# Attention and two squared-ReLU MLPs on one core: the product of probabilities and values in whole 128-row key blocks

## The chip, the core and the metric

The kernel runs on one core of a Trainium2 chip. Its engines are TensorE (PE in the profile; its weight loads stand as PEld), VectorE (DVE), ScalarE (ACT), GpSimd (POOL) and SyncE (SP), which here issues most of the DMAs. The metric is the device time of one execution in microseconds (us); lower is better.

## The reference

Four batches of eight heads, 576 positions, 64 dimensions per head, all in float32. Attention is causal with a decay, and two MLPs follow, each with 512 inputs, 2048 hidden units and a squared ReLU, over 2304 tokens:

```python
cum = np.cumsum(np.log(np.clip(f, 0.0001, 1.0)), axis=-1)
scores = np.matmul(q, k.transpose(0, 1, 3, 2)) / np.sqrt(D) + cum[:, :, :, None] - cum[:, :, None, :]
scores = np.where(causal, -1000000000.0, scores)
attn = np.exp(scores - np.max(scores, axis=-1, keepdims=True))
attn = attn / (np.sum(attn, axis=-1, keepdims=True) + 1e-09)
x = np.matmul(attn, v)            # then tokens x 512
h = np.maximum(x @ w_in, 0.0); x = h * h @ w_out       # first MLP
r = np.maximum(x @ w_in2, 0.0); out = r * r @ w_out2   # second MLP
```

## The kernel before, in words

The kernel first writes all its work as operations with an engine, an estimated duration, a priority and what they depend on (`op`, line 88), and a list scheduler (`Plan.run`, line 106) simulates the engines and puts out the instructions in the order that it finds. Each engine then works its own queue in that fixed order, with semaphores between them. A change of an estimated duration can therefore change the order on every engine, from the simulated moment on in which the operation is first placed.

The queries of a batch are cut at 0, 64, 192, 320, 448 and 576 (`QB`, line 19). Queries 0 to 191 are done first, in small products (lines 485 to 627). The other 384 queries of a head are one `unit` (line 634), 32 in all, in three query tiles of 128 (t = 2, 3, 4). A unit loads q and k, splits them into high and low parts on ScalarE, VectorE and GpSimd (lines 649 to 665), makes scores on TensorE (line 704), takes the maximum (line 408), the exponential (line 416), normalizes and splits the probabilities into two float16 parts (lines 431 and 438) and lays them out in `ph` as 2 x `NB` blocks of 128 queries by 128 keys, 13 for each part: blocks 0 to 3 for query tile 2, 4 to 7 for tile 3, 8 to 12 for tile 4 (`PB`, line 22). A query tile ends 64 positions into a key block, so its last key block is half used: the upper 64 keys lie after every query of the tile, and the lower 64 after the first 64 queries, whose probabilities there are zero by the mask. `consts_ph` (line 1311) fills the upper halves with zeros once, at the start. A DMA from the queue of SyncE (line 722) transposes all blocks into `pt`, of which there is one buffer (`npt=1`): keys on partitions, queries along the free side.

`av` (line 727) multiplies the values with them. The values are in `vv` as three bfloat16 parts; the first two stand side by side as 128 columns of weights, so that one matmul gives both products in the two halves of the output's partitions. For each key block j there are "cuts": the half block of the query tile for which j is the last (64 rows, 64 to 128 of its query columns), and the full block for all later query tiles (128 rows). Each cut is one matmul with the high and one with the low part of the probabilities. Then the cuts are taken once more for the third part of the values with the high part of the probabilities alone: 64 columns of weights, which write to the lower or the upper 64 partitions of the output, as `THIRD` (line 26) says. The values of keys 576 to 639 are zeros (line 1467). All add up in one PSUM bank; ScalarE and VectorE add its halves into `X` (line 752).

The first MLP (`hidden`, line 850; `mlp_a`, line 888) takes groups of 256 tokens, sixteen pieces of the hidden units each: 12 matmuls of 256 columns per piece for the first product (line 848) and 12 for the second (line 923). These fill TensorE between the heads' products, and go on alone when the last head is done. From the end of attention on, VectorE, ScalarE and GpSimd prepare the second MLP's weights (lines 1043 to 1116), which TensorE then works (lines 1220 and 1246).

The steps that matter most below are the transpose (`o_tr`, line 724: after the probabilities, with a free `pt`) and the product (`o_av`, line 750: after the transpose and the values, holding `pt`, `vv` and the output bank).

Of the kernel before, what the change touches and what calls it, by code (L numbers as in the profile page):

```python
# [18 lines left out]
QB = [0, 64, 192, 320, 448, 576]  # L19
Q0, QA = QB[1:3]  # L20

PB = {2: 0, 3: 4, 4: 8}
NB = 13
MW = 448

THIRD = ((0, 0), (1, 1), (3, 1), (5, 0), (2, 0), (4, 0), (6, 1))
S15 = 2.0 ** -15


# [40 lines left out]
class Plan:  # L70
# [17 lines left out]
    def op(self, eng, dur, fn, prio, deps=(), uses=(), data=None, other=None, dmas=1, rows=128):  # L88


        o = Op()
        o.how, o.uses, o.data, o.dmas, o.rows, o.turn = {eng: (dur, fn, 0)}, tuple(uses), data, dmas, rows, dur == self.TURN[0]
        if other:
            o.how[other[0]] = (other[1], other[2], 1)
        o.prio = (prio, len(self.ops))
        o.outs, o.ready, o.nwait = [], 0.0, 0
        for d in deps:
            if d is not None:
                d.outs.append(o)
                o.nwait += 1  # L100
        for b in o.uses:
            b.left += 1
        self.ops.append(o)
        return o
# [122 lines left out]
def act(n, psum=False):  # L227
    return (0.052 if psum else 0.093) + 0.00083 * n
# [6 lines left out]
def dve2(n):  # L235
    return Port(0.07 + n / 1920.0)
# [26 lines left out]
def attention_then_two_squared_relu_mlps(  # L263
# [16 lines left out]
    B, H, D2, S = qk.shape  # L280
# [10 lines left out]
    op = P.op  # L291
# [66 lines left out]
    def groups(c0, c1):  # L358
        return range(max(c0, 0) // GA, (c1 - 1) // GA + 1)
# [82 lines left out]
    def v_parts(vv, n, prio, dep):  # L442


        def rest(eng, i):
            x = vv()[:, :, i]
            eng.tensor_tensor(out=vv()[:, :, 1] if i == 0 else x.bitcast(BF16)[:, :, 0::2], in0=x,  # L447
                              in1=x.bitcast(BF16)[:, :, 1::2], op=ALU.subtract)

        for i in range(2):  # L450
            dep = either(TUNE["vr"], ("POOL", pool_(n * D), lambda i=i: rest(nc.gpsimd, i)),
                         ("DVE", dvs(n * D), lambda i=i: rest(nc.vector, i)), prio, [dep], [vv_of[vv]])
        return dep
# [180 lines left out]
    def unit(b, h, prio, first):  # L634

        c = QA
        qk_ = [Buf(QK), Buf(QK)]
        ta, tb = qk_
        raw, vv, ph, pT, o = Buf(RAW), Buf(VV), Buf(PH), Buf(PT), Buf(BO)
# [50 lines left out]
        ov = op("SP", P.COPY[0], load_v, prio + TUNE["vd"], [ld], [vv], data=0.91)  # L690
        ov = v_parts(vv, 5, prio + TUNE["vd"], ov)

        p_ops = []
        for t, blk in PB.items():
            pp = Buf(PP)
            q0, wd = QB[t], QB[t + 1]
            cuts = [(0, wd)] if wd <= 512 else [(0, wd // 2), (wd // 2, wd)]
# [26 lines left out]
        o_tr = op("SP", P.TURN[0], tr, prio, p_ops + (a_av if b == 0 else []), [ph, pT], data=2.9)  # L724


        def av():
            x, w_, z = pT(), vv().bitcast(BF16), o()
            cuts = []
            for j in range(5):  # L730
                if j >= 2:
                    cuts.append((j, min(128, QB[j + 1] - 128 * j), slice(128 * j - QA, QB[j + 1] - QA), (slice(PB[j] + j, PB[j] + j + 1), slice(64, 128))))
                t = max(2, j + 1)
                if t <= 4:
                    cuts.append((j, 128, slice(QB[t] - QA, S - QA), (slice(PB[t] + j, PB[4] + j + 1, 4), slice(0, 128))))
            todo = []
            for j, rows, q, (n, c) in cuts:
                for z0 in range(0, 2 * NB, NB):
                    todo.append((z[:, q], w_[:rows, j].rearrange("p z d -> p (z d)")[:, 1::2], x[:rows, n.start + z0:n.stop + z0:n.step or 1, c]))
            for i, half in THIRD:  # L740
                j, rows, q, (n, c) = cuts[i]
                todo.append((z[64 * half:64 * half + 64, q], w_[:rows, j, 1, 0::2], x[:rows, n.start:n.stop:n.step or 1, c]))
            for i, (dst, lt, rh) in enumerate(todo):
                nc.tensor.matmul(dst.rearrange("p (n c) -> p n c", n=rh.shape[1]), lhsT=lt, rhs=rh, start=(i == 0), stop=(i == len(todo) - 1),  # L744
                                 skip_group_check=True)


        p0, p1 = pos(b, QA), pos(b, QA) + S - QA
        gone = [y for g in groups(p0 - RING, p1 - RING) for y in split_x_ops[g][h // 2]] if p1 > RING else []
        o_av = op("PE", 2.06, av, prio, [o_tr, ov] + gone, [pT, vv, o])  # L750

        def fold(eng):
            s = p0
# [516 lines left out]
    with tc.manual_schedule():  # L1270
# [46 lines left out]
        def f_clip(a, z):  # L1317
            nc.vector.tensor_scalar(out=f_in[:, a:z], in0=f_in[:, a:z], scalar1=1.0e-4, scalar2=1.0, op0=ALU.max, op1=ALU.min)

        def f_ln(a, z):  # L1320
            nc.scalar.activation(out=f_log[:, a:z], in_=f_in[:, a:z], func=AF.Ln)
# [42 lines left out]
        o = op("SP", P.COPY[0], f_load, U, data=0.2)  # L1364
# [9 lines left out]
        o = op("DVE", dve2(Q0), lambda: f_clip(0, Q0), U, [o_f])  # L1374
        o = op("ACT", act(Q0), lambda: f_ln(0, Q0), U, [o])
# [7 lines left out]
        o = op("DVE", 0.67, scan1, -1.0e7, [o_f])  # L1383
# [22 lines left out]
        for h in range(H):  # L1406
            unit(0, h, TUNE["BP0"] + TUNE["BP1"] * h, [step(TUNE["P10"] + TUNE["P11"] * h)] if TUNE["P10"] >= 0 else [])
        mlp_a(3)
        for h in range(H):
            unit(1, h, 4500.0 + 100.0 * h, [step(TUNE["P20"] + TUNE["P21"] * h)])  # L1410
        mlp_a(4)
        mlp_a(5)
        for h in range(H):
            unit(2, h, 6000.0 + 100.0 * h, [step(TUNE["P30"] + TUNE["P31"] * h)])
# [19 lines left out]
        gone, taken, far = [[] for _ in RIGHT], [], []  # L1434
        waiting, sums = None, []
        for u in range(NU):
# [14 lines left out]
            gone = [[x] for x in prods]  # L1451
# [55 lines left out]
```

## Time and profile before

| | before |
|---|---|
| time, median of 3 runs | 990.28 us (989.86 to 993.13) |
| span of the profiled execution | 990.6 us |
| TensorE busy | 966.4 us (98%), 6699 matmuls |
| VectorE busy | 687.9 us (69%) |
| ScalarE busy | 452.7 us (46%) |
| GpSimd busy | 340.2 us (34%) |
| line 744 (`av`) on TensorE | 77.7 us, 672 matmuls |
| mean granted clock of TensorE | 0.985 of 2.4 GHz |

The profiled execution's span agrees with the median to 0.3 us. Busy time counts an engine as busy while any of its instructions runs. Matmuls are pipelined: the next one starts before the one ahead of it has ended, so the durations of single matmuls can't be added up, and the distance from start to start is what one costs. A line of the timeline gives a start, the length from there to the end of the last of its matmuls, and how many there are; looked at through a narrow window it gives the start of a single matmul.

### The profile page before, as it was taken

To read this page: it belongs to the slowest core of one execution; us is meant where nothing else is said; L and a number is where in the kernel's file an instruction comes from. 1 tells how busy PE (TensorE), PEld (TensorE's weight loads), DVE (VectorE), ACT (ScalarE), POOL (GpSimd) and SP (SyncE) were. 2 spreads that over 40 slices of the span, in tenths; PEclk is the share of its full clock that TensorE was granted. 3 is DMA by queue.
4 is the path that set the end of the run, shared out by engine and by line. 5 is a ranking of instruction groups with operands and counts; after the bars stand their busy time and mean duration, and the time that the engine had idled before them with its cause. 6 is when DMAs were issued, how large, how long until landed. Compare 5 with 4: busy or idle time off the path is not lost.

```text
span 990.6 us, 17537 instructions
## 1 busy us (share of the span) xinstructions
PE 966.4 (98%) x6699; PEld 864.2 (87%) x6699; DVE 687.9 (69%) x1351; ACT 452.7 (46%) x890; POOL 340.2 (34%) x278
## 2 busy tenths in 40 slices
PE   5999999999999999999999999999999999999997
PEld 3788898788888888888899999888898989899886
DVE  6989667767677777777378689979684445745343
ACT  2775577767677776766333344132231102311011
POOL 2211253444444344444222445343342213522220
PEclk6999999999999999999999999999999999999999
DMA  9766145656657655755557712863352211322223
GB/s 268 241 194 215 64 109 115 146 106 145 137 110 148 143 121 107 164 106 117 119 159 229 228 40 86 273 219 107 128 161 106 74 64 65 106 86 82 67 65 106
DMA packets 172948, 131.92 MB, mean 133 GB/s; under 512 B 134784, under 2 KB 151424, under 8 KB 170688
## 3 DMA queue, kind: packets, MB, share of 16 engines
q1 hardware_dynamic: 172608, 130.32, 48.4%
q8 instruction: 52, 0.85, 0.3%
q10 hardware_dynamic: 256, 0.49, 0.2%
q14 instruction: 32, 0.26, 0.1%
HBM read 85.07 MB, written 18.42 MB: 104 GB/s over the span
## 4 chain that ended last, share of the span: by engine, by line
PE 74%; issue 8%; DVE 7%; DMA 4%; POOL 2%; ACT 2%; SPq 1%; POOLq 0%; DVEq 0%; ACTq 0%
PE hp L848 17%; PE yp L923 16%; PE hp L1220 12%; PE bk L1246 10%; PE bk L744 7%; PE yp L1246 5%; PE bk L704 4%; POOL g L1233 2%; DVE w L1109 1%; DMA st<-in_w_dram 1%; PE bk L617 1%; DMA w<-wo_d 1%; PE bk L577 1%; DMA ph<-in_w_dram 1%; PE bk L619 1%
## 5 line engine op out<-in xcount | busy, mean ns | idle before, releaser
L923 PE MATMUL yp<-gt,w 128*128 128x256 f32 x1728 | 229.6, 282 | 1.6 <-POOL gt L873 1.6
L848 PE MATMUL hp<-xk,w 128*128 128x256 f32 x1728 | 225.9, 281 | 0.0
L923 PEld LDWEIGHTS yp<-gt,w 128*128 128x128 f32 x1728 | 215.9, 189 | 3.4 <-POOL gt L873 2.0
L848 PEld LDWEIGHTS hp<-xk,w 128*128 128x128 f32 x1728 | 213.6, 188 | 1.0 <-DVE xk L542 0.2
L873 POOL TENSOR_TENSOR gt<-sq,gt 128x512 fp32r<-128x512 f32 x72 | 100.1, 1390 | 202.2 <-ACT gt L870 189.0
L1246 PE MATMUL bk<-w,g 128*128 128x512 f32 x576 | 148.3, 394 | 0.4 <-DMA w<-wo_d 0.2
L1233 POOL TENSOR_TENSOR g<-r,g 128x768 fp32r<-128x768 f32 x36 | 66.6, 1851 | 212.1 <-ACT g L1232 210.3
L1220 PE MATMUL hp<-w 128*128 128x384 f32 x630 | 123.8, 335 | 0.3 <-DVE st L1197 0.3
L1232 ACT CAST g<-r 128x768 fp32r<-128x768 f32 x47 | 39.3, 836 | 184.1 <-DVE r L1231 184.0
L1246 PEld LDWEIGHTS bk<-w,g 128*128 128x128 f32 x576 | 106.6, 188 | 18.3 <-POOL g L1233 0.6
L1220 PEld LDWEIGHTS hp<-w 128*128 128x128 f32 x630 | 111.6, 188 | 8.3 <-DVE st L1197 0.7
L416 ACT ACTIVATE pp<-pp,stat 128x448 f32<-128x448 f32 (+1 forms) x128 | 78.5, 614 | 42.8 <-DVE stat L408 34.8
L438 DVE SCALAR_TENSOR_TENSOR ph<-pp,stat,ph 128x320 f16<-128x320 f32 (+2 forms) x96 | 76.2, 798 | 13.9 <-ACT ph L431 12.7
L1197 DVE TENSOR_TENSOR r<-hp,st 128x384 f32<-128x384 f32 x62 | 34.4, 555 | 66.1 <-PE hp L1220 65.6
L744 PE MATMUL bk<-pt,vv 64*128 64x64 f16 (+7 forms) x672 | 77.7, 253 | 0.0
L447 POOL TENSOR_TENSOR vv<-vv 128x320 f32<-128x320 f32 x64 | 55.7, 871 | 55.0 <-DMA vv<-in_v_dram 47.5
L1220 PE MATMUL hp<-w,far 128*128 128x384 f32 x378 | 74.4, 335 | 0.0
L1246 PE MATMUL yp<-w,g 128*128 128x512 f32 x288 | 74.4, 393 | 0.0
L1231 DVE SCALAR_TENSOR_TENSOR r<-r 128x768 f32<-128x768 f32 x47 | 73.0, 1553 | 1.4
L857 ACT ACTIVATE sq<-hp 128x512 f32<-128x512 f32 x72 | 42.9, 596 | 67.4 <-PE hp L848 66.1
L1220 PEld LDWEIGHTS hp<-w,far 128*128 128x128 f32 x378 | 67.3, 188 | 4.9
L744 PEld LDWEIGHTS <-vv 128*128 128x128 bf16 (+3 forms) x672 | 37.1, 101 | 38.8 <-issue 24.9
(174 smaller groups left out, 1269.9 us busy)
## 6 DMA issues: line engine op xcount, KB each, us to landing
w<-wo_d SPq DMA_DIRECT2D x48, 512.0 KB
stage<-in_w_dram SPq DMA_DIRECT2D x26, 512.0 KB
raw<-in_qk_dram SPq DMA_DIRECT2D x32, 288.0 KB
wo_d<-part SPq DMA_DIRECT2D x16, 512.0 KB
st<-in_w_dram SPq DMA_DIRECT2D x7, 1024.0 KB
ph<-in_w_dram SPq DMA_DIRECT2D x7, 1024.0 KB
vv<-in_v_dram SPq DMA_DIRECT2D x32, 160.0 KB
qk_a<-in_qk_dram SPq DMA_DIRECT2D x16, 192.0 KB
```

The source lines that it names most:

```text
L416: nc.scalar.activation(out=x, in_=x, func=AF.Exp, scale=-1.0, bias=nmax[:rows, t:t + 1], accum_out=ssum[:rows, t:t + 1])
L438: nc.vector.scalar_tensor_tensor(out=flat[:rows, z:z + wd], in0=x, scalar=r, in1=flat[:rows, 128 * blk:128 * blk + wd], op0=ALU.mult, op1= ...
L447: eng.tensor_tensor(out=vv()[:, :, 1] if i == 0 else x.bitcast(BF16)[:, :, 0::2], in0=x, in1=x.bitcast(BF16)[:, :, 1::2], op=ALU.subtract)
L744: nc.tensor.matmul(dst.rearrange("p (n c) -> p n c", n=rh.shape[1]), lhsT=lt, rhs=rh, start=(i == 0), stop=(i == len(todo) - 1), skip_grou ...
L848: nc.tensor.matmul(ps, lhsT=lt, rhs=rh, start=(k_ == 0 and c == 0), stop=(k_ == KD - 1 and c == 2))
L857: nc.scalar.activation(out=sq()[:, :c], in_=ps()[:, :c], func=AF.Relu)
L873: eng.tensor_tensor(out=gt[1]()[:, :c], in0=sq()[:, :c], in1=f32(gt[0]()[:, :c]), op=ALU.subtract)
L923: nc.tensor.matmul(yp[d // 2]()[:, d % 2], lhsT=lt, rhs=rh, start=(i == 0 and c == 0 and d % 2 == 0), stop=(i == NF - 1 and c == 2), skip_ ...
L1220: nc.tensor.matmul(ps()[:, 0:TH], lhsT=lt, rhs=rh, start=(k_ == 0 and c == 0), stop=(k_ == 1 and c == 2))
L1231: o = op("DVE", dvs(TU), lambda r=r: nc.vector.scalar_tensor_tensor(out=r(), in0=r(), scalar=0.0, in1=r(), op0=ALU.max, op1=ALU.mult), e0, ...
L1233: l = either_vp(TU, lambda e, r=r, g=g: e.tensor_tensor(out=g()[:, 1], in0=r(), in1=f32(g()[:, 0]), op=ALU.subtract), e0, [h], [r, g])
L1246: nc.tensor.matmul(bank(ob[c]), lhsT=g()[:, a, c * 128:(c + 1) * 128], rhs=rw()[:, b], start=(p == 0 and x == 0 and z == 0), stop=(p == NP ...
```

## The change

A key block's half piece and its full piece become one cut with all 128 rows: key block 2 goes over all 384 query columns, block 3 over the last 256 and block 4 over the last 128. Where a half block has no probabilities, the zeros that lie in `pt` are multiplied. There are five cuts instead of seven kinds of pieces, so a head has 15 matmuls instead of 21. The third part's list is rewritten for the five cuts: blocks 0, 3 and 4 write to the lower 64 partitions, blocks 1 and 2 to the upper ones. The planner is told 1.65 us for the operation instead of 2.06.

```diff
-THIRD = ((0, 0), (1, 1), (3, 1), (5, 0), (2, 0), (4, 0), (6, 1))
+THIRD = ((0, 0), (1, 1), (3, 0), (2, 1), (4, 0))
...
             for j in range(5):
-                if j >= 2:
-                    cuts.append((j, min(128, QB[j + 1] - 128 * j), slice(128 * j - QA, QB[j + 1] - QA), (slice(PB[j] + j, PB[j] + j + 1), slice(64, 128))))
-                t = max(2, j + 1)
-                if t <= 4:
-                    cuts.append((j, 128, slice(QB[t] - QA, S - QA), (slice(PB[t] + j, PB[4] + j + 1, 4), slice(0, 128))))
+                t = max(2, j)
+                cuts.append((j, slice(QB[t] - QA, S - QA), slice(PB[t] + j, PB[4] + j + 1, 4)))
             todo = []
-            for j, rows, q, (n, c) in cuts:
+            for j, q, n in cuts:
                 for z0 in range(0, 2 * NB, NB):
-                    todo.append((z[:, q], w_[:rows, j].rearrange("p z d -> p (z d)")[:, 1::2], x[:rows, n.start + z0:n.stop + z0:n.step or 1, c]))
+                    todo.append((z[:, q], w_[:, j].rearrange("p z d -> p (z d)")[:, 1::2], x[:, n.start + z0:n.stop + z0:n.step]))
             for i, half in THIRD:
-                j, rows, q, (n, c) = cuts[i]
-                todo.append((z[64 * half:64 * half + 64, q], w_[:rows, j, 1, 0::2], x[:rows, n.start:n.stop:n.step or 1, c]))
+                j, q, n = cuts[i]
+                todo.append((z[64 * half:64 * half + 64, q], w_[:, j, 1, 0::2], x[:, n]))
...
-        o_av = op("PE", 2.06, av, prio, [o_tr, ov] + gone, [pT, vv, o])
+        o_av = op("PE", 1.65, av, prio, [o_tr, ov] + gone, [pT, vv, o])
```

## Rows read from the trace of the kernel before

**Rows 1.** The page: the span of the profiled execution.
```profile
span 990.6 us, 17537 instructions
```

**Rows 2.** Busy time by stage: stretch, length, busy us of each engine, clock, DMA.
```profile
165.00:200.00 35.00, 32.72 (x257) 28.38 (x256) 26.26 (x74) 25.87 (x56) 15.88 (x15) 0.95 0.68 138
200.00:475.00 275.00, 274.89 (x2277) 242.10 (x2276) 204.10 (x557) 196.14 (x403) 114.96 (x109) 1.00 0.62 130
492.00:575.00 83.00, 83.00 (x706) 82.96 (x705) 61.50 (x85) 26.70 (x46) 26.14 (x19) 1.00 0.58 185
575.00:620.00 45.00, 43.09 (x330) 41.76 (x330) 40.93 (x53) 22.16 (x34) 23.00 (x15) 1.00 0.24 74
```

**Rows 3.** TensorE's timeline through one head's product: start us, length us, what, count.
```profile
217.95 0.29 PE L704 MATMUL bk<-qk 68*128 68x288 f32 x1
218.09 0.34 PE L744 MATMUL bk<-pt,vv 128*128 128x384 f16 x1
...
218.59 0.33 PE L744 MATMUL bk<-pt,vv 128*128 128x384 f16 x1
218.85 0.23 PE L744 MATMUL bk<-pt,vv 64*128 64x64 f16 x2
219.01 0.28 PE L744 MATMUL bk<-pt,vv 128*128 128x256 f16 x1
219.13 0.27 PE L744 MATMUL bk<-pt,vv 128*128 128x256 f16 x1
219.33 0.39 PE L744 MATMUL bk<-pt,vv 64*128 64x64 f16 x3
219.50 0.29 PE L744 MATMUL bk<-pt,vv 128*128 128x128 f16 x2
219.56 0.38 PE L744 MATMUL bk<-pt,vv 128*128 128x128 f16 x3
219.72 0.23 PE L744 MATMUL bk<-pt,vv 64*128 64x64 f16 x2
219.88 0.35 PE L744 MATMUL bk<-pt,vv 128*64 128x384 f16 x2
220.06 0.28 PE L744 MATMUL bk<-pt,vv 128*64 128x128 f16 x2
220.27 0.25 PE L744 MATMUL bk<-pt,vv 64*64 64x64 f16 x3
220.45 0.39 PE L848 MATMUL hp<-xk,w 128*128 128x256 f32 x1
```

**Rows 4.** Busy time of line 744 alone, whole span: matmuls, weight loads.
```profile
sum 1000.00, PE 77.72 PEld 37.05; mean PE 77.72 PEld 37.05
```

**Rows 5.** TensorE's timeline where whole-array matmuls go over to 64-column ones.
```profile
38.67 0.28 PE L848 MATMUL hp<-xk,w 128*128 128x256 f32 x1
38.90 0.32 PE L617 MATMUL bk<-pt,vv 128*64 128x128 f32 x1
```

**Rows 6.** Groups by line and shape: count, busy us, mean ns, idle before.
```profile
L744 PE MATMUL bk<-pt,vv 64*128 64x64 f16 x192 | 22.1, 196 | 0.0
```

**Rows 7.** Transposes on SyncE's queue, and the start of one head's product.
```profile
220.55 3.99 SPq L722 DMA_TRANSPOSE pt<-ph  x1
231.27 3.93 SPq L722 DMA_TRANSPOSE pt<-ph  x1
317.54 3.94 SPq L722 DMA_TRANSPOSE pt<-ph  x1
325.01 0.34 PE L744 MATMUL bk<-pt,vv 128*128 128x384 f16 x1
```

**Rows 8.** The chain that ended last, around the fourth head: start, length, what.
```profile
170.05 4.20 DMA raw<-in_qk_dram
181.67 2.25 PE hp L848 x12
183.92 2.12 PE yp L923 x12
```

## The prediction

> **What bounds the kernel now.** I began with the span [rows 1] and with busy time by stage [rows 2]. In the attention stage, from 200 to 475 us, TensorE is covered for 274.89 of 275.00 us, VectorE for 204.10 and ScalarE for 196.14. From 492 to 575 us, where only products of the first MLP are left, TensorE has all 83.00 us. From 575 to 620 us it has 43.09 of 45.00 and VectorE 40.93: here the second MLP's weights are prepared, and the two are nearly level. The granted clock is 1.00 in these three, so TensorE runs at 2.4 GHz. In the one stage that the change touches, TensorE's queue is the limit; nothing else is nearer than 204 of 275.
>
> A busy share doesn't tell whether TensorE works or waits inside an instruction, so I next read one head's product of probabilities and values start by start [rows 3]. Its 21 matmuls take from 218.09 to 220.45, 2.36 us. The busy time of line 744, 77.72 us over 672 matmuls [rows 4], is 2.43 us a head for 32 heads; that counts the tail of each head's last matmul, which lies over the next operation's start, so 2.36 stands for all heads. In these 2.36 us the reader is to look at differences between starts:
> - full 128-row matmuls of 384 columns: four starts over 0.50 us (218.09 to 218.59), 0.167 each;
> - the last of them before a 64-row piece: 0.26 (218.59 to 218.85), 0.095 more for the same columns;
> - a pair of 64-row pieces with 64 columns: 0.16 (218.85 to 219.01), 0.17 (219.33 to 219.50), 0.16 (219.72 to 219.88), where the streaming of 128 columns at 0.167 for 384 is 0.06. So each pair carries about 0.1 us as well, on its way back to 128 rows;
> - 256 columns: 0.12 (219.01 to 219.13), and 0.20 (219.13 to 219.33) ahead of a piece; 128 columns: 0.06 and 0.16;
> - the third value part, two 64-column halves of the array at once: 0.18 (219.88 to 220.06) for 384 columns on both halves, then 0.21, then 0.18 for three 64-row pieces.
>
> So 0.095 us is lost at each change of the array's shape, and not where the width changes: scores with 68 rows and 288 columns go over to 128 rows and 384 columns in 0.14 us (217.95 to 218.09, the first two of [rows 3]), which is 288 columns at the same rate and 0.015. From 128 columns of the array to 64 (line 848 to line 617) a matmul of 256 columns takes 0.23 [rows 5] where one like it took 0.12, so that change costs 0.11.
>
> **The change part by part.** *Removed:* three pairs of 64-row pieces and, of the third value part, three pieces; in all nine matmuls of 64 columns a head (the 192 of [rows 6] are six for each of 32 heads, the x3 near the end of [rows 3] is the other three), and with them six of eight changes of shape: to 64 rows and back behind block 1 and behind block 2 (four), the 64 rows between block 3 and the halves (one), and the 64 rows between the halves and the next operation (one). *Added:* zeros. Blocks 2, 3 and 4 take 384, 256 and 128 columns with all 128 rows, where they took 256, 128 and none beside the pieces. *After*, each term from rows 3:
> - blocks 0 to 2, six matmuls of 384 columns, 6 x 0.167 = 1.00;
> - block 3, two of 256: 0.12 as read, or 0.11 by columns (256/384 x 0.167), as the one read stood behind a change; 0.22 for both;
> - block 4, two of 128: 0.06, and 0.16 ahead of a change of shape, 0.22;
> - third part: blocks 0 and 1 on the two halves 0.18; then block 2's 384 columns on one half beside blocks 3 and 4 (256 + 128) on the other. A 384 ahead of a change costs 0.26, and the second matmul on the same half starts about 0.02 late (0.18 against 0.16 of columns): 0.28.
>
> The sum is 1.00 + 0.22 + 0.22 + 0.46 = 1.90 us, 0.46 less than 2.36; 32 x 0.46 = 14.7 us. Bounds: if block 4's matmul on its half starts only when the other half has ended, the last term is 0.18 + 0.16 = 0.34, and with 0.12 and 0.08 for the two uncertain starts a head takes 2.00: 11.5 us. If the 0.167 is really the 0.165 of 218.26 to 218.59 and the change to halves is no dearer than 0.09, a head takes 1.87: 15.7 us. I stay near the middle, since each term has a row of its own shape.
>
> For the 128-column starts the Trainium skill (TensorE: Matmul & The Clock Gate, section "Back-to-back issue gap") gives about 81 ns for each matmul with its weight load. The row shows 0.06 us; by the page's figure the saving would be 0.6 us smaller in all (an estimate, 0.02 x 32), and the row decides.
>
> A rule speaks against the change: the Trainium skill (TensorEngine Tiling (Array Packing), section "Performance Considerations") would keep a contraction of 64 rows as a 64-row tile, two running side by side. Here both pieces of a pair lie on the same 64 rows and start 0.03 to 0.04 us apart, one after the other. If they did run together, that would be worth at most 0.04 x 3 x 32 = 3.8 us to the old form, while its changes of shape would stay, so the rule doesn't turn the sum.
>
> *Where the time goes next.* One transposed buffer serves all heads, so the next head's transpose starts when this product ends: at 220.55, just behind 220.45 [rows 3, 7]. It therefore moves up with the shorter product, and the pitch, 10.72 us from 220.55 to 231.27, becomes 10.26. Between two products TensorE has 10.72 - 2.36, some 8.3 us, of scores and MLP products; the transpose at 317.54 was in use at 325.01, after 7.47 us [rows 7], so it is covered with the same work as before. VectorE's 204.10 of 275.00 [rows 2] would become 78% of a stretch shorter by 4.3%: still cover. The preparation from 492 us starts at the last head's end, and the last group's products move up too, so the level stage of 575 to 620 us moves as a whole; nothing in the program starts at a fixed time. The sum goes against 990.6 us of the profiled execution [rows 1], which is 0.3 us above the median of 990.28: 990.28 - 14.7 = 975.6.
>
> *The planned duration.* The diff also tells the list scheduler 1.65 instead of 2.06 us, and the order on every engine is written from its simulated times. Up to the first head's product nothing moves. Behind it the order is decided by what is ready at the end of that product, and the distances from there are the same, so I expect five MLP products between two heads as now. A cost on its own I put at nothing, with bounds of one stall either way: the only large one in the stage is between the third and the fourth head [rows 8], where a late load (170.05, 4.20 us) made TensorE wait; 35.00 - 32.72 = 2.28 us idle [rows 2], and two products then took 2.25 and 2.12 instead of 1.42 at the lower clock (1.2 GHz; 0.95 is the mean of that stretch), 1.5 us more. One stall is thus 3.8 us.
>
> **The rivals.**
> 1. *New stalls from a shifted order*, one or two of 3.8 us, in the attention stage or where VectorE is level with TensorE (575 to 620 us): 979 to 983. For it: 40.93 of 45.00. Against: the whole stage moves together.
> 2. *The stall before the fourth head vanishes* with the new order: 972. For it, it hangs on one queue order; against, the load follows the transpose and moves up with it.
> 3. *The gap belongs to a change of width, not of shape.* Then 384 to 256 and 256 to 128 still pay 0.095 each, 0.19 x 32 = 6.1 us: 981.7. Against: the 68-row scores, which change width at 0.015.
> 4. *Slower:* the new order leaves four MLP products between two heads instead of five. Then TensorE's cover is 8.3 - 1.4 = 6.9 us (twelve starts of 0.12, [rows 3, 5], are 1.4), and each head waits for its transpose from 0.6 (landing at 7.47) up to 1.3 us (8.2). At 0.6 it takes 24 of the 32 heads, at 1.3 it takes 11, to eat the 14.7 us; if all 32 do, the time is 995 to 1017. Against: the fifth product is taken because it is ready while the transpose is not, and neither time hangs on the product's length.
> 5. *The change doesn't do what it says:* were the zero blocks no longer whole, the count of matmuls at line 744's successor would not fall to 480.
>
> **How the numbers follow.** Forecast (973.5 to 978) 0.70; rival 1 0.14; rival 2 0.08; rival 3 0.03; rival 4 0.03; the rest, an effect I don't see, 0.02. The time is the forecast's, 975.6. The range of 970 to 983 holds the forecast with both bounds of the sum (974.6 to 978.8), rivals 1 and 2, and rival 3. A measurement of this kernel can tell about 0.3% (3 us) from no change: faster 0.94, within it 0.02, slower 0.04.
>
> **What would show it.** In the profile after: 480 matmuls at the product's line, none of 64 rows; starts of a head over 1.87 to 1.95 us; no 0.095 gap between blocks 1 and 2 or 2 and 3, one between block 4 and the halves; pitches of 10.2 to 10.3 us; the last head ending some 15 us sooner, and the start of the second MLP with it. Wrong would be: a head above 2.0 us (the halves serialize, or width matters), or TensorE below full cover between 200 and 475 us (the order shifted).

## The result

The changed kernel takes 977.07 us (median; 976.36 to 977.69) beside 990.59 us for the kernel before (median of four runs): ratio 0.9865, 95% interval 0.9845 to 0.9884. That is 13.5 us less; 975.6 was forecast. The sign, the place and nearly the size are as forecast, but the experiments show that two errors of the prediction partly cancel in this: the product gained 1.4 us more than it said, and what the other engines make of that, and of the planned duration, is not nothing but some 2.6 us.

The page of the changed kernel, its first two rows (three lines of the program fewer, so line 744 is now 741, 848 is 845 and 923 is 920):

```profile
span 975.9 us, 17152 instructions
...
PE 951.1 (97%) x6507; PEld 863.0 (88%) x6507; DVE 681.9 (70%) x1352; ACT 451.5 (46%) x889; POOL 340.1 (35%) x278
```

TensorE has 192 matmuls fewer, six for each of 32 heads. Busy time by stage (stretch, its length, then PE, PEld, DVE, ACT and POOL busy, clock, DMA share, GB/s), to be read beside [rows 2]:

```profile
165.00:200.00 35.00, 35.00 (x288) 32.67 (x288) 27.77 (x78) 27.82 (x58) 16.07 (x15) 1.00 0.71 149
200.00:475.00 275.00, 271.64 (x2172) 248.00 (x2171) 206.14 (x558) 195.16 (x402) 116.10 (x111) 0.99 0.63 129
```

From 165 to 200 us TensorE is now never idle, where 2.28 us were missing. From 200 to 475 us it is idle for 3.36 us, where 0.11 were missing. Over both stretches that is 3.36 us for 2.39: the one large stall of the scores moved from the fourth head to a later one. TensorE's timeline, before and then after (in brackets the idle time ahead of the start, and what ended it):

```profile
181.14 0.54 PE L704 MATMUL bk<-qk 128*128 128x288 f32 x2 [1.93 <-DVE stat L408]
```

```profile
307.33 1.09 PE L704 MATMUL bk<-qk 128*128 128x288 f32 x4 [1.48 <-DVE stat L408]
```

The granted clock is 0.50 (1.2 GHz) behind each of the two, from 182 to 185 us before and from 309 to 312 us after, so this cost moved with the stall.

One head's product, TensorE's timeline through narrow windows (start, length to the end of the last one, what, count), beside [rows 3]:

```profile
202.82 0.34 PE L741 MATMUL bk<-pt,vv 128*128 128x384 f16 x1
...
203.81 0.38 PE L741 MATMUL bk<-pt,vv 128*128 128x256 f16 x2
203.91 0.39 PE L741 MATMUL bk<-pt,vv 128*128 128x256 f16 x3
204.02 0.28 PE L741 MATMUL bk<-pt,vv 128*128 128x128 f16 x2
204.08 0.50 PE L741 MATMUL bk<-pt,vv 128*128 128x128 f16 x3
204.23 0.35 PE L741 MATMUL bk<-pt,vv 128*64 128x384 f16 x2
204.42 0.33 PE L741 MATMUL bk<-pt,vv 128*64 128x256 f16 x3
204.68 0.40 PE L704 MATMUL bk<-qk 128*128 128x288 f32 x1
```

Six matmuls of 384 columns take 0.99 us, two of 256 take 0.21, two of 128 take 0.21, the third part 0.45: 1.86 us from 202.82 to 204.68, where 2.36 stood. Two losses at a change of shape are left, both forecast: the one before the halves, at 204.08 (0.15 for 128 columns, where 0.06 stands ahead of it), and the one from the halves back to the next operation, in the 0.26 from 204.42 to 204.68.

What the transposes and the scores show is not as forecast. Transposes on SyncE's queue, beside [rows 7]:

```profile
388.34 3.93 SPq L722 DMA_TRANSPOSE pt<-ph  x1
398.61 4.30 SPq L722 DMA_TRANSPOSE pt<-ph  x1
...
449.90 4.39 SPq L722 DMA_TRANSPOSE pt<-ph  x1
461.69 3.89 SPq L722 DMA_TRANSPOSE pt<-ph  x1
```

Some pitches are about the forecast's 10.26 us (388.34 to 398.61), others are longer, up to 11.8 (449.90 to 461.69). Counted from the trace, 161 MLP pieces (12 matmuls each) now lie between the first and the last head's product instead of 156; 24 of the 31 gaps have five (27 before), the others three, six or seven. The line of the products and that of the scores, with what the latter waited for (us, times; the waits of matmuls and of weight loads are both counted and overlap, so such lists are compared only with each other), first before, then after:

```profile
L744 PE MATMUL bk<-pt,vv x672: 190/219/352, 151.8 to 491.3; 64*128 64x64 f16 x48, 128*128 128x384 f16 x32, 64*64 64x64 f16 x24, 128*128 128x256 f16 x16
...
  DVE stat L408: 5.3, 5
  DMA qk<-aug_d: 0.9, 2
  DVE qk L665: 0.5, 2
```

```profile
L741 PE MATMUL bk<-pt,vv x480: 218/326/544, 149.9 to 483.6; 128*128 128x384 f16 x64, 128*128 128x256 f16 x32, 128*128 128x128 f16 x32, 128*64 128x256 f16 x32
...
  DVE stat L408: 7.1, 12
  DMA qk<-aug_d: 1.7, 4
  DVE ph L438: 0.6, 1
  DVE qk L665: 0.5, 1
```

The last matmul of the last head's product starts only 7.6 us sooner (491.3 to 483.6), not 15, and 1.9 us of that had passed ahead of the first product (151.8 to 149.9), where the change has no part: from 0 to 149 us the granted clock is 0.92 in the trace of before and 0.95 in the one after. The other traces below begin the first product between 148.8 and 150.9. Set from the first product to the end of the span, the traces differ by 838.8 - 826.0 = 12.8 us. The products account for 32 x 0.50 = 16.1 us of gain; 3.3 us were given back. Of these 0.7 lie inside the products of two heads that were held up (0.4 in the one at 311.5 us, which began at the lower clock), and 2.6 in the distances between other starts from the first to the last product. I call a start late by what its distance from the one ahead of it exceeds the median distance of that pair of lines and shapes in all traces; these sum to 6.7 us before and 9.3 after, 1.5 of the difference at the scores and 1.0 at the MLP's products.

### The profile page after: what moved, and what is told of

It reads as the page before. It is cut to its first block, busy times and chain, and to the rows that moved or that the text cites. A ratio compares the mean times of both kernels' runs of the same rounds, so it can differ in the third digit from the quotient of the medians.

```text
span 975.9 us, 17152 instructions
## 1 busy us (share of the span) xinstructions
PE 951.1 (97%) x6507; PEld 863.0 (88%) x6507; DVE 681.9 (70%) x1352; ACT 451.5 (46%) x889; POOL 340.1 (35%) x278
## 4 chain that ended last, share of the span: by engine, by line
PE 72%; issue 9%; DVE 9%; DMA 3%; POOL 3%; ACT 3%; SPq 1%; POOLq 0%; DVEq 0%; ACTq 0%
PE yp L920 16%; PE hp L845 16%; PE hp L1217 13%; PE bk L1243 10%; PE bk L741 5%; PE yp L1243 5%; PE bk L704 4%; POOL g L1230 2%; DMA st<-in_w_dram 1%; DVE w L1106 1%; PE bk L617 1%; DMA qk<-aug_d 1%; PE bk L577 1%; DVE ph L438 1%; DVE tmp L805 1%
## 5 line engine op out<-in xcount | busy, mean ns | idle before, releaser
L408 DVE CUSTOM_DVE_ANT_0 pp<-bk,mask 128x448 f32<-128x448 f32 (+1 forms) x128 | 59.8, 475 | 13.2 <-PE bk L704 10.2
L857 DVE SCALAR_TENSOR_TENSOR sq<-hp,sq 128x512 f32<-128x512 f32 x64 | 44.0, 688 | 35.2 <-ACT sq L854 34.8
```

Of the source, the lines that this page charges most:

```text
L408: nc.vector.tensor_tensor_reduce(out=x[:rows, c0:c0 + wd], in0=src, in1=msk, scale=-0.125, scalar=3.0e38 if first else nmax[:rows, 5:6], o ...
```

## The experiments

All ratios are against the kernel before, run beside each kernel on its chip. The clock doesn't separate these kernels: the mean granted clock of each one's runs lies between 0.988 and 0.991, which is worth some 2 us between the extremes (an estimate: 0.002 of 980), and in each of the traces of before, after, e1, e2 and e3 it falls to 1.2 GHz once between the first and the last product. The theory that I began with: the product gained all 16.1 us, and the changed order lost some of it. Its rival: the order costs nothing, and the shorter product itself exposes a wait.

### The order of before with the new product, and the reverse

e1 changes only the planned duration of the changed kernel back:

```diff
-        o_av = op("PE", 1.65, av, prio, [o_tr, ov] + gone, [pT, vv, o])
+        o_av = op("PE", 2.06, av, prio, [o_tr, ov] + gone, [pT, vv, o])
```

> The five whole-block cuts, but the planner is told 2.06 us as before, so every engine's order is that of the kernel before. If the part of the gain that is missing (32 heads x 0.50 us are 16.1 us, 13.5 came) was lost to the changed order: a head's product 1.86 us, 156 MLP pieces between the first and the last head as before, no new stalls, 974.5 us, about 2.5 us less than the changed kernel (ratio 0.984). If the missing part belongs to the shorter product itself (less work to cover the next head's transpose): about 977 us, ratio 0.9865, with waits at the products.

Measured: ratio 0.9914 (0.9901 to 0.9927), 980.15 us, a gain of only 8.5 us. A head's product takes 1.86 us and 156 pieces lie between the heads, as in the kernel before. My theory falls: with the old order, more of the gain is lost (7.6 us of 16.1), not less. The list of what the scores waited for in e1:

```profile
  DVE stat L408: 8.6, 17
  DVE qk L665: 4.1, 5
```

VectorE's part is 12.7 us where it was 5.8 (5.3 + 0.5) in the kernel before, in the same order of instructions. Line 408 takes the maximum out of the scores' PSUM bank and so frees it; line 665 copies a part of q. Both stand in VectorE's queue, and TensorE now comes back to the scores half a microsecond sooner after each head.

e2 has the kernel before with 1.65 us planned:

```diff
-        o_av = op("PE", 2.06, av, prio, [o_tr, ov] + gone, [pT, vv, o])
+        o_av = op("PE", 1.65, av, prio, [o_tr, ov] + gone, [pT, vv, o])
```

> The old cuts with 64-row pieces, but the planner is told 1.65 us, so the order is that of the changed kernel. If the changed order costs time by itself: a head's product still 2.36 us, 161 MLP pieces between the first and the last head instead of 156, and some 2.7 us more than the kernel before, 993.3 us (ratio 1.003). If the order costs nothing: 990.6 us.

Measured: ratio 1.0026 (1.0012 to 1.0040), 161 pieces, a head's product 2.36 us. As expected, the new order by itself costs some 2.6 us. Its trace doesn't show that at the scores: VectorE's part of their waits is 5.6 us, no more than before; where the 2.6 us go was not followed. So the four kernels are: old product and old order 1, new product and old order 0.9914, old product and new order 1.0026, new product and new order 0.9865. In the new order the product's 16.1 us are gained in full as far as the intervals tell (1.0026 - 0.9865 = 0.0161, 16 us, give or take 2.4); in the old order half of them. VectorE's part of the waits fits that: the shorter product adds 2.6 us to it in the new order (5.6 to 8.2), 6.9 in the old one (5.8 to 12.7).

### What the old order waits for

e5 is e1 with less work on VectorE and the same order: of the first MLP's squares in the attention stage it does the left half and leaves out the other.

```diff
         def square():
+            h = c // 2 if 26 <= idx < 106 else c
             nc.vector.scalar_tensor_tensor(
-                out=sq()[:, :c], in0=ps()[:, :c], scalar=0.0, in1=sq()[:, :c], op0=ALU.max, op1=ALU.mult)
+                out=sq()[:, :h], in0=ps()[:, :h], scalar=0.0, in1=sq()[:, :h], op0=ALU.max, op1=ALU.mult)
```

> As e1 (whole blocks, 2.06 us planned, order of the kernel before), but VectorE squares only the left half of the first MLP's hidden units in the attention stage (pieces 26 to 105 of 144; part of the MLP is left out, the order of all engines is the same). That takes about 0.3 us from each of 40 squares, some 12 us of VectorE's 205 in that stage. If e1's scores wait for VectorE because TensorE now comes back sooner: the waits at the scores (line 704) shrink by 3 us or more of e1's 11, and the time falls from ratio 0.991 to about 0.987. If the lost part of the gain lies elsewhere (transposes, DMA, GpSimd): as e1, 0.991.

> The control: the kernel before with the same half squares left out. If VectorE is no limit with the long product: the waits at the scores (line 704), 5.7 us before, fall by 1 to 2 us at most, ratio 0.998 to 1.000. If VectorE limits the attention stage in any case: a gain as large as e5 has over e1.

> The changed kernel (whole blocks, 1.65 us planned) with the same half squares left out. If its order already gives VectorE the time it needs: a smaller gain than e5 over e1, 0.985 after 0.9865. If VectorE is what the changed order waits for as well: 0.983 or less.

Measured: e5 0.9859 (0.9845 to 0.9872), the control e6 0.9988 (0.9979 to 0.9997), e7 0.9851 (0.9837 to 0.9864). The same relief of VectorE is worth 5.5 thousandths on e1, 1.2 on the kernel before and 1.4 on the changed kernel (not clear of the intervals). Busy time from 200 to 475 us (columns as above), e1 and then e5:

```profile
200.00:475.00 275.00, 271.84 (x2191) 249.12 (x2190) 205.79 (x555) 198.05 (x407) 120.12 (x111) 1.00 0.65 131
```

```profile
200.00:475.00 275.00, 273.46 (x2212) 251.42 (x2211) 195.95 (x552) 197.50 (x405) 119.96 (x112) 1.00 0.65 133
```

What the scores waited for in e5, and then in the control e6:

```profile
  DVE stat L408: 5.6, 8
  DVE qk L665: 3.3, 4
```

```profile
  DVE stat L408: 3.8, 3
  DMA qk<-aug_d: 1.4, 3
  DVE qk L665: 0.6, 1
```

VectorE's part falls from 12.7 to 8.9 in e5, from 5.8 to 4.4 in the control. e1 lost 7.7 thousandths of the product's gain (16.1 us are 16.3, of which 8.6 came), and the relief gives back 5.5, that is 4.3 more than the control gets; the granted clock rose along (by 0.002 from e1 to e5, each against the kernel before beside it, by 0.001 in the control), so about 1 of the 4.3 may be the clock's (an estimate). So VectorE's queue takes a large part of what the old order loses, though VectorE is busy for only 75% of the stretch: a share leaves open whether one operation is late for one wait. That it takes all of it isn't shown. The squares stand in the MLP's own chain too, but by the traces the gain doesn't come that way: the scores' starts are late by 5.0 us in all before, 9.7 in e1 and 6.8 in e5, those of the MLP's two products by 1.7, 2.0 and 2.2.

### Is it the change of shape, or the small matmul?

e3 keeps all 21 matmuls and the 64 columns of the pieces, with 128 rows; planned duration and order of before:

```diff
-                    cuts.append((j, min(128, QB[j + 1] - 128 * j), slice(128 * j - QA, QB[j + 1] - QA), (slice(PB[j] + j, PB[j] + j + 1), slice(64, 128))))
+                    cuts.append((j, 128, slice(128 * j - QA, QB[j + 1] - QA), (slice(PB[j] + j, PB[j] + j + 1), slice(64, 128))))
```

> All 21 matmuls stay, the pieces keep their 64 query columns, but take all 128 rows, zeros included; planned duration and order as before. If the time lies in changes of the array's shape: only two are left, a piece costs 0.03 to 0.04 us, a head 1.70 to 1.78 us, that is less than with whole blocks since 448 columns fewer stream, and the kernel takes 970 to 972 us (ratio 0.980). If small matmuls themselves are dear (weight load and start for 64 columns): a head stays at 2.2 us or more, 985 us or more.

Measured: a head's product 1.68 us, a little under the 1.70 to 1.78 expected, and ratio 0.9893 (0.9878 to 0.9907), 978 us: the product as the theory of shapes has it, the time not. TensorE's timeline around the pieces of one head of e3:

```profile
224.11 0.44 PE L744 MATMUL bk<-pt,vv 128*128 128x64 f16 x4
224.14 0.41 PE L744 MATMUL bk<-pt,vv 128*128 128x64 f16 x3
224.17 0.38 PE L744 MATMUL bk<-pt,vv 128*128 128x256 f16 x2
224.28 0.39 PE L744 MATMUL bk<-pt,vv 128*128 128x256 f16 x4
```

A piece costs 0.03 us, no more than its columns, where a pair cost 0.16 and the matmul ahead of it 0.09 more. So small matmuls aren't dear; the six changes of shape were the whole loss (0.674 us a head, 0.11 for each), and the rival of the width is refuted, since the width goes from 384 to 64 and to 256 within these lines. Nor are 64 rows dear by themselves: of the two 64-row pieces at 218.85 [rows 3] the first costs 0.04 us, and only the one ahead of the change pays. The weight loads of the same stretches show what a change does, first before, then e3:

```profile
218.84 0.28 PEld L744 LDWEIGHTS <-vv 64*128 64x128 bf16 x4 [0.32 <-issue]
```

```profile
223.95 0.43 PEld L744 LDWEIGHTS <-vv 128*128 128x128 bf16 x5
```

In e3 each load starts as the matmul ahead of its own starts. At a change the load isn't taken ahead: before, the loads pause for 0.32 us, until the first 64-row load starts at 218.84, just as its own matmul does (218.85). Whether the 0.095 us is that load's wait or the matmul's is not shown.

The 21.6 us that e3's products save (32 x 0.674) came to 10.7: VectorE's part of the scores' waits is 16.4 us (8.7 + 5.8 + 1.9), which points to the same loss as in e1, larger:

```profile
  DVE stat L408: 8.7, 20
  DVE qk L665: 5.8, 8
  POOL vv L447: 2.3, 6
  DVE stat L422: 1.9, 1
```

e4 puts two changes of shape back into e1: the last key block with 64 rows.

```diff
-                    todo.append((z[:, q], w_[:, j].rearrange("p z d -> p (z d)")[:, 1::2], x[:, n.start + z0:n.stop + z0:n.step]))
+                    r = 64 if j == 4 else 128
+                    todo.append((z[:, q], w_[:r, j].rearrange("p z d -> p (z d)")[:, 1::2], x[:r, n.start + z0:n.stop + z0:n.step]))
...
-                todo.append((z[64 * half:64 * half + 64, q], w_[:, j, 1, 0::2], x[:, n]))
+                r = 64 if j == 4 else 128
+                todo.append((z[64 * half:64 * half + 64, q], w_[:r, j, 1, 0::2], x[:r, n]))
```

> As e1 (five cuts, 2.06 us planned), but the last key block's matmuls (128 columns, two and one) take 64 rows, as the upper 64 rows hold only zeros. Columns and count stay as in e1. If the shape's changes cost 0.095 us each: two more a head (to 64 rows ahead of the halves, and to 64 rows inside the halves), a head 2.05 us, 6.1 us above e1, 980.6 us. If width, count or zeros set the time: as e1, 974.5 us.

Measured: a head's product 2.13 us, ratio 0.9962 (0.9952 to 0.9973). The product is longer by 0.28 us, more than the 0.19 expected. TensorE's timeline of one head:

```profile
226.69 0.27 PE L743 MATMUL bk<-pt,vv 128*128 128x256 f16 x1
226.90 0.28 PE L743 MATMUL bk<-pt,vv 64*128 64x128 f16 x2
226.97 0.50 PE L743 MATMUL bk<-pt,vv 64*128 64x128 f16 x3
227.11 0.36 PE L743 MATMUL bk<-pt,vv 128*64 128x384 f16 x2
227.30 0.33 PE L743 MATMUL bk<-pt,vv 128*64 128x256 f16 x2
227.56 0.24 PE L743 MATMUL bk<-pt,vv 64*64 64x128 f16 x1
227.73 0.39 PE L922 MATMUL yp<-gt,w 128*128 128x256 f32 x1
```

The first change costs 0.21 - 0.11 = 0.10 ahead of 226.90 and 0.01 behind it, as said. The second costs 0.17: the last 64-row matmul no longer runs beside the 384 columns of the other half, but begins 0.26 behind them and takes its own 0.17. That is the term that I had left out. The time rose by 4.8 thousandths over e1, 4.7 us, where 32 x 0.28 are 8.8: it looks like the reverse of e1's loss, the longer product covering VectorE's work again (VectorE's part of the waits is 7.3 us, 5.6 + 1.7, after 12.7).

### Is 1.65 us a good plan, or a lucky one?

> The 64-column pieces with all 128 rows (e3), but the planner is told 1.65 us, close to the 1.68 us that e3's trace shows. If a planned duration near the real one is what lets the other engines follow the shorter product: 21.6 us of product less than before (32 x 0.674) and waits as in the changed kernel, 5 to 6 us below e3, about 971 us, ratio 0.982 to 0.984, the fastest kernel. If the order is a matter of luck: as e3, 0.989, or worse.

e8 is e3 with 1.65 us planned. Measured: 972.93 us, ratio 0.9832 (0.9818 to 0.9845), the fastest kernel here, 3.3 thousandths under the changed one; VectorE's part of the waits fell from 16.4 to 9.2 us. That agreed with the idea that a plan near the real duration helps, so I tested it at the changed kernel with its real duration, and at a shorter one:

> The changed kernel with the duration that its trace shows, 1.86 us, in the plan. If a plan nearer to the real duration brings the gain (1.65 and 2.06 are each 0.2 away, and gave ratios 0.9865 and 0.9914): waits at the scores below 7.1 us and 973 to 975 us, ratio 0.984 or less. If the figure only shuffles a list order, with no direction: anything between 0.984 and 0.992.

> The changed kernel with 1.45 us in the plan, 0.4 below the real duration. If nearness to the real duration decides: worse than 1.65, as bad as 2.06 or worse (0.990). If a shorter planned product makes the planner bring scores late enough for VectorE to follow, whatever the real one is: 0.986 or less. If it is a shuffle: anything between 0.984 and 0.992.

> The 64-column pieces with 128 rows, 1.45 us in the plan (1.65 gave 0.9832 with a real product of 1.68 us). Nearness: worse than 0.9832, about 0.986. A shorter plan is better as such: 0.982 or less. A shuffle: no order to be seen against e10.

| planned us | whole blocks (real 1.86) | 64-column pieces, 128 rows (real 1.68) |
|---|---|---|
| 1.45 | 0.9924 (0.9908 to 0.9940), e10 | 0.9898 (0.9880 to 0.9916), e11 |
| 1.65 | 0.9865 (0.9845 to 0.9884), the change | 0.9832 (0.9818 to 0.9845), e8 |
| 1.86 | 0.9979 (0.9967 to 0.9991), e9 | |
| 2.06 | 0.9914 (0.9901 to 0.9927), e1 | 0.9893 (0.9878 to 0.9907), e3 |

The idea falls: the plan with the real duration is the worst. There is no direction in the figure; from 0.9865 to 0.9979 are 11 us, nearly as much as the change gained, and 0.9979 lies even outside what I had given for a shuffle. The two columns move together, and a plan has the same count of MLP pieces in every gap in both (156 in all with 2.06, 161 with 1.65, 159 with 1.45), so it is the order that counts and not a chance of the runs. What the scores waited for in e9, and the longest entries of TensorE's matmul waits there (the program's order, by line; us in total, times, longest):

```profile
  DVE stat L408: 9.8, 18
  DVE qk L665: 4.2, 7
```

```profile
PE bk L704 <- DVE stat L408: 3.3, 5, 1.4
PE bk L704 <- DMA qk<-aug_d: 2.8, 2, 2.3
PE yp L920 <- POOL gt L870: 2.4, 4, 1.3
```

The places are the ones of e1 and two more of VectorE's (lines 422 and 425, 3.5 us), with a late load of the decay rows (`aug_d`) and GpSimd's split of the hidden units besides. Why the planner lays the loads and VectorE's queue worse with one figure than with another was not followed, and stays open.

## Why the prediction was right, and where it was wrong

- *TensorE's queue is the limit of the stage:* right for the kernel before. For the kernel after it holds less: the scores wait for VectorE's queue as well, which its share (75% from 200 to 475 us, 78% by the prediction) didn't show.
- *The cost lies in changes of the array's shape, not of width:* right, shown by e3 (a piece without a change costs 0.03 us) and e4 (a change put back costs 0.11 us, and 0.17 where it also ends the running side by side).
- *The sum of 1.90 us a head:* a little high; 1.86 was measured, 0.50 saved instead of 0.46, 16.1 us instead of 14.7. The terms were 0.99, 0.21, 0.21 and 0.45 for 1.00, 0.22, 0.22 and 0.46: the first start of a run, 0.01 dearer than the next ones, had been put into each.
- *VectorE "still cover":* wrong. It was argued from a busy share of a stretch, while the scores already waited on VectorE in the kernel before. In the order of before, half of the gain is lost, a large part of it here (e1, e5 and the control), where the prediction allowed it nothing.
- *The planned duration at nothing, five pieces between two heads, an unchanged order:* wrong, and this is the step that failed most. The order changed (161 pieces, up to seven in a gap). Had it stayed, as I expected, the time would have been e1's 980 us, outside the forecast's band of 973.5 to 978, though inside the range of 970 to 983. The bounds that I had put on it, one stall of 3.8 us either way, were too narrow: the plan's figure is worth 11 us. With 1.86 in the plan the same matmuls take 986.9 us, outside the range. That 1.65 is the best of the four figures tried was not foreseen, so that the time came out near the forecast is in part luck.
- *Rivals 1 and 2* both came true, as one stall that moved: the one ahead of the fourth head is gone (35.00 of 35.00 us covered from 165 to 200), and a like one came at 307 us, with some smaller ones (3.36 us idle from 200 to 475). The prediction put the first down to a late load, with which the chain begins; by the profile VectorE's maximum (line 408) ended the wait in both. Rival 3 is refuted by e3. Of rival 4, no gap with four pieces is in the changed kernel (one has three), and no head waited for its transpose by more than 0.1 us. Rival 5: there are 480 matmuls, all with 128 rows.
- *The last head 15 us sooner:* wrong, 7.6, as five MLP pieces moved ahead of it. It cost nothing to speak of, since they were missing behind it: the first MLP's last product, TensorE's own work, still started its last matmul 15.7 us sooner (611.8 to 596.1), 1.9 of them from ahead of the first product.

## What to carry to other kernels

Where matmuls of different row or column extents alternate in one TensorE queue, read the distance from start to start at each change: here 0.1 us each, so that, for these products, multiplying zeros in whole blocks was much cheaper than leaving them out with 64 rows, and the cheapest was to leave out columns and keep the rows. A gain on the engine that bounds a stage may be worth its full size only where the next engine's queue follows, as here it did not in the old order; look for waits on that engine that are there already, however small, and not at its busy share. Where a list scheduler writes the order, a planned duration is part of the change: run the change with the old figure and the old code with the new one before either is given the credit.

## What the runs showed of the hardware that I had not expected

A matmul of 64 columns and 128 rows costs 0.03 us among others of its shape, just its columns, weight load included, though the load's record is about 0.1 us long. Ahead of a change of shape the next load doesn't start early, and 0.095 us is lost (e3 beside the kernel before). A change to 64 rows inside the two-halves shape costs more than the change alone: 0.17 us for 128 columns, since the matmul also loses its place beside the other half.
